# Two half batches by head parity, one transfer per unit of w_in and per phi, K or V load, and new sizes in the plan

## The chip, the core and the metric

The kernel runs on one core of one Trainium2 chip. The metric is the time of one execution in device microseconds (us); of the kernel before three runs are known, 734.42, 734.64 and 735.23, with the median 734.64. Five engines work side by side: TensorE (PE, its weight loads PEld), VectorE (DVE), ScalarE (ACT), GpSimd (POOL) and SyncE (SP), which here only issues transfers. A transfer runs on the core's 16 DMA engines.

## The reference

```
# q, k, v: 8 x 8 x 576 x 64, phi: 8 x 8 x 576 x 32   (batch, head, token, ...)
a    = softmax of phi over the tokens
k_m  = einsum('bhsm,bhsd->bhmd', a, k)          # 32 x 64 per head
v_m  = einsum('bhsm,bhsd->bhmd', a, v)
attn = softmax(q @ k_m.T / 8)                   # 576 x 32 per head
x    = (attn @ v_m), heads side by side         # 4608 x 512
h    = x @ w_in                                 # w_in 512 x 2048
out  = (relu(h) ** 2) @ w_out                   # w_out 2048 x 512
```

The weights w_in and w_out arrive as 64-bit floats, so each is 8 MB. The other inputs are 32-bit.

## The kernel before, in words

**The mathematics is folded.** Since x is attn times v_m, the kernel never forms x: it multiplies v_m by w_in once per batch (VW, function `vw`) and then h is attn times VW. `attention_turned` (batches 0 and 1) and `attention` (2 to 7) make attn, turned so that the memory slots lie on the partitions, as a high part `ath` and a rest `atl`. `mm1` makes h as three products (high by high, rest by high, high by rest), 12 matmuls of 288 columns for one slice of 128 columns of w_in; ACT and DVE make relu and square, again as a high part `gh` and a rest `glo`. `mm2` adds the slice to four accumulators, 12 matmuls of 512 columns; `mm2_left` does the left-over 64 tokens of two batches. There are 16 slices in each of 8 batches. Slices go first through 4 of batch 0, then the 16 of batch 1, then the other 12 of batch 0, then batch 2 and on.

**The weights.** `decode` loads a unit of 128 rows by 512 numbers (0.52 MB in 64 bit) into a buffer `raw` and makes 32-bit floats with some six DVE and ACT instructions. There are 16 units of w_in (`piece("wi", j)`, four for each quarter j) and 16 of w_out. The units of w_in come as two transfers, one to partitions 0 to 63 and one to 64 to 127, since a tile holds heads 0 to 3 in its lower 64 partitions and heads 4 to 7 in its upper 64. Units of w_out come as one transfer to 128 partitions.

**The inputs of a batch.** Batches 0 and 1 are computed in two halves of four heads (`memory_half`, hh 0 and 1), with tokens on the partitions; phi, K, V and q of a half come as a transfer to 128 partitions and a small one for the left-over 64 tokens. In batches 2 to 7 `memory` loads phi, K and V with `rows`, two transfers of 64 partitions each.

**The order of the work.** Every step is recorded as an operation with the engines that may do it and a cost. `Plan.order` gives each operation a rank from the table PLACES and plays the program through with these costs; the start times that come out set the order in which each engine's instructions are written, and which engine does a step where it has a choice. A load counts its `size` as time on the wire, `size / WIRE`, after FIRST ns. Where the play leaves TensorE idle, `emit` writes `fill` matmuls of 512 columns on zeros, one for each 260 ns of the gap: into a bank nobody reads (L472), or adding zero to a live accumulator (L474). The fills do no work of the reference. Waits at run time are by semaphores; each engine does its instructions in the order written, and SP issues the transfers in the order written as well.

The first h of the program (`h_0`, batch 0) needs `ath` and `atl` of both halves, that is: q of the second half, its scores `psc`, its softmax on DVE and ACT, a transpose `pat` and two evictions. It also needs VW of the first quarter of w_in, that is its four units.

Of the kernel before, what the change touches and what calls it, by code (L numbers as in the profile page):

```python
# [27 lines left out]
FIRST = 1100  # L28
# [360 lines left out]
def tile_attention_moe(  # L389
# [90 lines left out]
    seq += [(b, f) for b in range(2, B) for f in range(NFF)]  # L480


    w_in_u = w_in.bitcast(U32).rearrange("(r s d) (f t) -> r d s f t", r=2, d=D, t=2)
    w_out_u = w_out.bitcast(U32).rearrange("(j p) (e t) -> p j e t", p=P, t=2)
    wi = {}
    wo = {}

    def decode(kind, j, h, room):
# [4 lines left out]
        def load(d):  # L493
# [3 lines left out]
            for r in (0, 1):  # L497
                d(R()[64 * r:64 * r + 64].rearrange("p (f t) -> p f t", t=2), w_in_u[r][:, h, j * ND:(j + 1) * ND, :])
# [652 lines left out]
```

## Time and profile before

| what | value |
|---|---|
| median of three runs | 734.64 us |
| the profiled execution, its own time | 732.51 us |
| its span on the core | 730.7 us |
| TensorE busy | 717.7 us, 98% |
| VectorE busy | 488.8 us, 67% |
| ScalarE busy | 323.0 us, 44% |
| granted TensorE clock, mean | 1.00 of full speed |
| read from memory, written | 56.10 MB, 9.44 MB |

The span runs from the first to the last instruction; 1.8 us of the profiled execution lie outside it. The share of TensorE holds the fill matmuls as busy time, and matmuls overlap in the pipeline, so that the mean of one is longer than the distance from one to the next. A share over the whole span hides that the program has two parts: until about 140 us weights are loaded and decoded, after that they are at hand.

### The profile page before, as it was taken

What the parts mean: (1) busy time and instruction counts of PE and PEld (TensorE: products, weight loads), DVE (VectorE), ACT (ScalarE), POOL (GpSimd) and SP (SyncE); (2) the same over time, 40 slices, a digit from 0 to 9 for tenths busy, and PEclk for the clock granted to TensorE, in tenths of its full rate; (3) what the DMA queues carried; (4) which work ended last, traced back from release to release, by engine and by line L of the source; (5) the groups of instructions that cost most, each with busy time, mean ns of one, the idle gap of its engine ahead of it and who ended that gap; (6) DMA issues with size and microseconds to landing.
All of it is one profiled execution on the core that took longest, in us unless ns stands there. A gap on an engine that the chain in (4) does not pass through costs nothing.

```text
span 730.7 us, 13856 instructions
## 1 busy us (share of the span) xinstructions
PE 717.7 (98%) x5440; PEld 580.5 (79%) x5445; DVE 488.8 (67%) x1153; ACT 323.0 (44%) x737; POOL 53.4 (7%) x116
## 2 busy tenths in 40 slices
PE   8899899999999999999999999999999999999997
PEld 4577688787788878888888888887888888888886
DVE  3899999943684559666884358855795357764541
ACT  3577997753551335323452235533443134343230
POOL 1000000010001000120004100040004100040000
PEclk9999999999999999999999999999999999999999
DMA  9995444496314342035304421145314010020002
GB/s 238 267 249 138 144 146 118 138 214 157 82 31 117 84 98 62 14 103 136 92 1 118 119 62 31 32 116 122 77 31 109 23 32 1 1 58 1 1 0 73
DMA packets 46241, 66.44 MB, mean 91 GB/s; under 512 B 9760, under 2 KB 33312, under 8 KB 46176
## 3 DMA queue, kind: packets, MB, share of 16 engines
q1 hardware_dynamic: 42144, 56.77, 30.9%
q0 software_dynamic: 3552, 8.13, 4.0%
q8 instruction: 43, 0.70, 0.4%
q10 hardware_dynamic: 480, 0.66, 0.3%
q14 instruction: 22, 0.18, 0.1%
HBM read 56.10 MB, written 9.44 MB: 90 GB/s over the span
## 4 chain that ended last, share of the span: by engine, by line
PE 84%; DVE 5%; DMA 2%; ACT 2%; issue 1%; SPq 0%; DVEq 0%; ACTq 0%
PE h L944 25%; PE acc L982 15%; PE acc L979 15%; PE acc L980 15%; PE accl L1005 6%; PE vwpv L836 4%; DMA raw<-in_moe_w_in_dram 2%; PE pkv_pa L593 1%; DVE work L512 1%; PE pscpa L876 1%; PE pkv_pv L593 1%; DVE work L520 1%; DMA raw<-in_moe_w_out_dram 1%; DVE work L511 0%; DVE work L509 0%
## 5 line engine op out<-in xcount | busy, mean ns | idle before, releaser
L944 PE MATMUL h<-ath,vw 128*128 128x288 f32 x1024 | 212.3, 296 | 0.5 <-ACT vw L446 0.5
L979 PE MATMUL acc<-wo,gh 128*128 128x512 f32 x512 | 203.8, 398 | 0.0
L980 PE MATMUL acc<-wo,gh 128*128 128x512 f32 x512 | 201.2, 393 | 0.0
L944 PEld LDWEIGHTS h<-ath,vw 128*128 128x128 f32 x1024 | 172.0, 188 | 19.4 <-ACT vw L446 1.4
L982 PE MATMUL acc<-wo,glo 128*128 128x512 f32 x512 | 181.1, 398 | 1.5 <-DVE glo L954 1.5
L950 ACT ACTIVATE gh<-r 128x512 fp32r<-128x512 f32 x128 | 80.6, 630 | 116.9 <-PE acc L980 81.0
L979 PEld LDWEIGHTS acc<-wo,gh 128*128 128x128 f32 x512 | 96.1, 188 | 28.0 <-issue 10.6
L982 PEld LDWEIGHTS acc<-wo,glo 128*128 128x128 f32 x512 | 93.8, 188 | 28.9 <-issue 9.6
L944 PE MATMUL h<-atl,vw 128*128 128x288 f32 x512 | 109.5, 295 | 0.0
L980 PEld LDWEIGHTS acc<-wo,gh 128*128 128x128 f32 x512 | 96.1, 188 | 16.5
L954 DVE TENSOR_TENSOR glo<-r,gh 128x512 fp32r<-128x512 f32 x128 | 87.5, 684 | 23.9 <-PE acc L982 19.1
L948 ACT ACTIVATE r<-h 128x288 f32<-128x288 f32 x146 | 58.7, 408 | 80.2 <-PE h L944 63.1
L949 DVE TENSOR_SCALAR r<-h 128x288 f32<-128x288 f32 x110 | 50.2, 456 | 64.0 <-PE h L944 62.3
L944 PEld LDWEIGHTS h<-atl,vw 128*128 128x128 f32 x512 | 82.1, 188 | 0.0
L1041 POOL DMA_DIRECT2D out_dram<-o x84 | 41.6, 502 | 476.1 <-DVE o L446 261.9
L953 DVE TENSOR_TENSOR r<-r 128x576 f32<-128x576 f32 x54 | 40.5, 758 | 40.7 <-ACT gh L950 30.8
L951 ACT ACTIVATE gl<-r 128x64 fp32r<-128x64 f32 x128 | 32.0, 252 | 58.0 <-DVE r L949 48.4
L952 ACT ACTIVATE r<-r 128x576 f32<-128x576 f32 x74 | 50.5, 685 | 1.6
L1005 PE MATMUL accl<-wo,gl 128*128 128x512 f32 x192 | 47.2, 393 | 0.0
L1005 PEld LDWEIGHTS accl<-wo,gl 128*128 128x128 f32 x192 | 35.6, 188 | 7.5
L955 DVE TENSOR_TENSOR gl<-r,gl 128x64 fp32r<-128x64 f32 x128 | 27.5, 218 | 9.5 <-ACT r L952 8.3
L446 ACT CAST vw<-vwpa 128x256 fp32r<-128x256 f32 x50 | 17.2, 377 | 32.0 <-PE vwpa L836 31.7
(157 smaller groups left out, 724.0 us busy)
## 6 DMA issues: line engine op xcount, KB each, us to landing
q<-in_q_dram SPq DMA_DIRECT2D x96, 136.0 KB, 2.9
raw<-in_moe_w_in_dram SPq DMA_DIRECT2D x32, 256.0 KB, 4.3
raw<-in_moe_w_out_dram SPq DMA_DIRECT2D x16, 512.0 KB, 3.5
out_dram<-o POOLq DMA_DIRECT2D x80, 64.0 KB, 2.9
KV<-in_v_dram SPq DMA_DIRECT2D x12, 320.0 KB, 6.6
KV<-in_k_dram SPq DMA_DIRECT2D x12, 320.0 KB, 6.3
phi<-in_phi_dram SPq DMA_DIRECT2D x12, 288.0 KB, 5.3
KV<-in_k_dram SPq DMA_DIRECT2D x12, 256.0 KB, 5.3
```

The costliest lines, as they stand in the source:

```text
L944: nc.tensor.matmul(p()[:, 0:n], V()[:, l, hh, c0:c0 + P], x()[:, hh, cs], start=(i == 0), stop=(i == 5))
L948: op({"ACT": act(n), **({} if b < 2 else {"DVE": tt(n)})}, lambda e, cs=cs, n=n, p=p: nc.scalar.activation(r()[:, cs], p()[:, 0:n], AF.Rel ...
L949: else nc.vector.tensor_scalar(r()[:, cs], p()[:, 0:n], 0.0, None, ALU.max), [p], [(r, h)])
L950: op({"ACT": act(SM)}, lambda e: nc.scalar.activation(gh(), r()[:, 0:SM], AF.Square), [r], [gh])
L952: op({"ACT": act(S), **({} if b < 2 else {"DVE": tt(S)})}, lambda e: nc.scalar.activation(r(), r(), AF.Square) if e == "ACT" else nc.vecto ...
L953: else nc.vector.tensor_mul(r(), r(), r()), [r], [r], port=BOTH)
L954: vec({"DVE": tt(SM)}, lambda e: nc.vector.tensor_sub(glo(), r()[:, 0:SM], gh().bitcast(F32)), [r, gh], [glo])
L979: nc.tensor.matmul(a(), gh()[:, c], t()[:, 0], start=f0, stop=False)
L980: nc.tensor.matmul(a(), gh()[:, c], t()[:, 1], start=False, stop=False)
L982: nc.tensor.matmul(a(), glo()[:, c], t()[:, 0], start=False, stop=f1)
L1005: nc.tensor.matmul(a(), G()[:, l, :], t()[:, w], start=(ff == 0 and n == 0), stop=(ff == NFF - 1 and n == 2))
L1041: d(rows, o()[32 * j:32 * (j + n), :])
```

## The change

The halves of a batch become the heads of one parity: half hh holds heads hh, hh + 2, hh + 4 and hh + 6 (`heads`). A pair of neighbouring heads then lies on partitions 0 to 63 and 64 to 127 of one tile. In w_in the 128 rows of two neighbouring heads are contiguous, and in phi, K and V so are their tokens; a unit of w_in and a load of phi, K or V in `memory` becomes one transfer to 128 partitions. Sizes in the plan are other numbers, FIRST goes from 1100 to 1400, and the table PLACES is new throughout. The arithmetic of every step stays as it was.

```diff
-FIRST = 1100
+FIRST = 1400
 PLACES = (
-    8, 1, 3, 9, 5, 15, 18, 19, 20, 21, ...
...
-    w_in_u = w_in.bitcast(U32).rearrange("(r s d) (f t) -> r d s f t", r=2, d=D, t=2)
+    w_in_u = w_in.bitcast(U32).rearrange("(s p) (f t) -> p s f t", p=P, t=2)
...
-            for r in (0, 1):
-                d(R()[64 * r:64 * r + 64].rearrange("p (f t) -> p f t", t=2), w_in_u[r][:, h, j * ND:(j + 1) * ND, :])
+            d(R().rearrange("p (f t) -> p f t", t=2), w_in_u[:, h, j * ND:(j + 1) * ND, :])
...
-        dma(load, 450000, w=[rk], two=kind == "wi", lead=True)
+        dma(load, 400000 if kind == "wi" else 335000, w=[rk], lead=True)
...
     def heads(x, b, hh):
 
-        return x[b, 4 * hh:4 * hh + 4]
+        return x[b].rearrange("(s r) n w -> r s n w", r=2)[hh]
 
     def rows(d, dst, src, lo, hi):
 
         w = src.shape[3]
-        for x in (0, 1):
-            d(dst[64 * x:64 * x + 64].rearrange("p h c w -> p h (c w)"),
-              src[0, 4 * x:4 * x + 4].rearrange("h (p c) w -> p h (c w)", c=RC)[:, :, lo * w:hi * w])
+        d(dst.rearrange("p h c w -> p h (c w)"),
+          src[0].rearrange("(s r) n w -> s (r n) w", r=2).rearrange("s (p c) w -> p s (c w)", c=RC)[:, :, lo * w:hi * w])
...
-        dma(lambda d: rows(d, a(), phi[b:b + 1], 0, RC), 807000, [], [A], two=True, lead=True)
+        dma(lambda d: rows(d, a(), phi[b:b + 1], 0, RC), 650000, [], [A], lead=True)
...
-        dma(lambda d: tokens(d, a(), heads(phi, b, hh)), 468000, [], [(A, (hh, "in"))], two=True, lead=True)
+        dma(lambda d: tokens(d, a(), heads(phi, b, hh)), 333000, [], [(A, (hh, "in"))], two=True, lead=True)
...
-            dma(load, 689000, [], [Q, QL], two=True, lead=True)
+            dma(load, 551000, [], [Q, QL], two=True, lead=True)
...
-                        src = q[b, 4 * hh + 2 * y:4 * hh + 2 * y + 2].rearrange("a (p c) d -> p a (c d)", c=NC)
+                        src = heads(q, b, hh)[2 * y:2 * y + 2].rearrange("a (p c) d -> p a (c d)", c=NC)
```

What the new plan does with the order is seen at three places. Line numbers after the change are two lower in most of the program. In all, the program has 79 fill matmuls before (74 ahead of the first h, 5 later) and 54 after, all ahead of the first h; all other matmuls are the same in number and shape. DVE has 14 instructions more and ACT 14 fewer, among them nine squares `r<-r` of batches 2 to 7 and six casts `vw<-vwpv` more on DVE.

SP, the start of the program, from the first half's inputs of batch 0 to the first unit of w_out; `KV_1` and `q_1` belong to the second half. Before:

```order
L498 DMA raw<-in_moe_w_in_dram 64x1024 x2
L639 DMA KV_1_84<-in_k_dram 128x4x256
L640 DMA KV_1_84<-in_k_dram 64x4x64
L639 DMA KV_1_84<-in_v_dram 128x4x256
L640 DMA KV_1_84<-in_v_dram 64x4x64
L752 DMA q_1_251<-in_q_dram 128x4x256
L753 DMA ql_1_253<-in_q_dram 64x4x64
L498 DMA raw<-in_moe_w_in_dram 64x1024 x4
L495 DMA raw<-in_moe_w_out_dram 128x1024
L639 DMA phi_350<-in_phi_dram 128x4x128
```

After:

```order
L497 DMA raw<-in_moe_w_in_dram 128x1024 x2
L637 DMA KV_1_86<-in_k_dram 128x4x256
L638 DMA KV_1_86<-in_k_dram 64x4x64
L637 DMA KV_1_86<-in_v_dram 128x4x256
L638 DMA KV_1_86<-in_v_dram 64x4x64
L497 DMA raw<-in_moe_w_in_dram 128x1024
L750 DMA q_1_256<-in_q_dram 128x4x256
L751 DMA ql_1_258<-in_q_dram 64x4x64
L495 DMA raw<-in_moe_w_out_dram 128x1024
L637 DMA KV_0_217<-in_k_dram 128x4x256
L638 DMA KV_0_217<-in_k_dram 64x4x64
L637 DMA phi_338<-in_phi_dram 128x4x128
```

All four units of the first quarter of w_in now stand ahead of `q_1`, where two stood before, and a K of batch 1 stands ahead of that batch's first phi.

DVE, the softmax of the second half of batch 0 (`rz_1`, `S_1`), shortly ahead of the first h; the row `work<-raw` belongs to the decoding of weights. Before:

```order
L667 TENSOR_TENSOR mx_0_437<-mx_0_437,phi_350 128x128
L446 CAST vw_0_462<-vwpv_0_443 128x256
L740 TENSOR_REDUCE rz_1_467<-S_1_453 128x16
L846 TENSOR_TENSOR vw_0_462<-vwpa_0_445,vw_0_462 128x256
L741 TENSOR_SCALAR rz_1_467<-rz_1_467 128x16
L846 TENSOR_TENSOR vw_1_465<-vwpa_0_445,vw_1_465 128x256
L846 TENSOR_TENSOR vw_0_462<-vwpv_0_443,vw_0_462 128x256
L511 TENSOR_SCALAR work<-raw 128x512
L742 RECIPROCAL rz_1_467<-rz_1_467 128x16
L846 TENSOR_TENSOR vw_1_465<-vwpv_0_443,vw_1_465 128x256
L743 TENSOR_TENSOR S_1_453<-S_1_453,rz_1_467 128x512
```

After:

```order
L665 TENSOR_TENSOR mx_0_438<-mx_0_438,phi_338 128x128
L844 TENSOR_TENSOR vw_0_445<-vwpa_0_427,vw_0_445 128x256
L736 TENSOR_TENSOR rest_208<-rest_208,redl_447 128x128
L738 TENSOR_REDUCE rz_1_454<-S_1_440 128x16
L844 TENSOR_TENSOR vw_1_456<-vwpa_0_427,vw_1_456 128x256
L739 TENSOR_SCALAR rz_1_454<-rz_1_454 128x16
L844 TENSOR_TENSOR vw_0_445<-vwpv_0_425,vw_0_445 128x256
L740 RECIPROCAL rz_1_454<-rz_1_454 128x16
L669 TENSOR_REDUCE mc_0_477<-pmx_0_474 128x1
L741 TENSOR_TENSOR S_1_440<-S_1_440,rz_1_454 128x512
```

A cast of VW, one subtraction of VW and an instruction of the decoding have left this stretch; the row on `rest` and the one on `mc_0` stood a little later before.

PE, the third VW of batch 0 (`vw_4`) and the first h that reads it. Before:

```order
L836 MATMUL vwpa_4_2229<-wi_1239,VT_221 32x512
L979 MATMUL acc_4_2_2090<-wo_1164,gh_2197 128x512
L980 MATMUL acc_4_2_2090<-wo_1164,gh_2197 128x512
L982 MATMUL acc_4_2_2090<-wo_1164,glo_2211 128x512
L474 LDWEIGHTS zero
L474 MATMUL acc_4_0_2080<-zero 128x512
```

After:

```order
L980 MATMUL acc_4_2_2042<-wo_1172,glo_2075 128x512
L980 MATMUL acc_4_0_2035<-wo_1133,glo_2179 128x512
L977 MATMUL acc_4_3_2046<-wo_1133,gh_2161 128x512
L978 MATMUL acc_4_3_2046<-wo_1133,gh_2161 128x512
L980 MATMUL acc_4_3_2046<-wo_1133,glo_2179 128x512
L977 MATMUL acc_4_1_2059<-wo_1133,gh_2161 128x512
L978 MATMUL acc_4_1_2059<-wo_1133,gh_2161 128x512
L980 MATMUL acc_4_1_2059<-wo_1133,glo_2179 128x512
L942 MATMUL h_1_2203<-ath_407,vw_4_2183 128x288 x2
```

Before, three matmuls of the second product and four fills, of which the first is shown, stand between the last matmul of VW and the h, and one more fill a little later. After, twelve matmuls of the second product stand there, of which the last eight are shown, and no fill.

## Rows read from the trace of the kernel before

**Rows 1.** The page: span, and busy time of each engine.

```profile
span 730.7 us, 13856 instructions
PE 717.7 (98%) x5440; PEld 580.5 (79%) x5445; DVE 488.8 (67%) x1153; ACT 323.0 (44%) x737; POOL 53.4 (7%) x116
```

**Rows 2.** Windows by stretch; columns in the first line.

```profile
core 0: us, PE busy (x) PEld busy (x) DVE busy (x) ACT busy (x) POOL busy (x), PEclk, DMA share, GB/s
0.00:40.60 40.60, 34.90 (x337) 19.46 (x341) 26.94 (x70) 16.90 (x35) 4.63 (x18) 1.00 0.99 256
40.60:75.00 34.40, 33.15 (x360) 26.29 (x359) 33.36 (x84) 28.32 (x66) 0.00 (x0) 1.00 0.68 173
75.00:140.00 65.00, 63.00 (x382) 51.78 (x374) 63.08 (x146) 56.07 (x126) 0.00 (x0) 1.00 0.50 145
...
182.00:725.00 543.00, 543.00 (x3980) 448.60 (x3979) 344.77 (x808) 200.36 (x463) 46.50 (x94) 1.00 0.24 61
```

**Rows 3.** Windows, fills of L472 alone: busy and count of PE, PEld.

```profile
0.00:40.60 40.60, 20.10 (x70) 7.78 (x74) 1.00 0.99 256
```

**Rows 4.** Timeline of PE: start, length in us, instruction, idle before it.

```profile
24.91 1.09 PE L764 MATMUL pq<-ident,q 128*128 128x128 f32 x8 [0.42 <-DMA q<-in_q_dram]
...
29.30 2.00 PE L792 MATMUL psc<-kb,qT 128*128 128x64 f32 x16 [1.28 <-ACT kb L446]
```

**Rows 5.** Timeline of PE, around the first h.

```profile
39.66 1.04 PE L472 MATMUL idle<-zero 128*128 128x512 bf16 x4
40.83 1.30 PE L687 MATMUL pkv<-KV,phi 128*32 128x128 f32 x40
```

**Rows 6.** DMA from 21 to 26.5 us: packets; queue, MB, share of engines.

```profile
DMA packets 404, 1.25 MB, mean 228 GB/s; under 512 B 83, under 2 KB 109, under 8 KB 403
...
q1 hardware_dynamic: 403, 1.24, 102.6%
```

**Rows 7.** DMA from 35 to 37 us, the same view.

```profile
DMA packets 231, 0.77 MB, mean 385 GB/s; under 512 B 33, under 2 KB 48, under 8 KB 231
...
q1 hardware_dynamic: 231, 0.77, 102.6%
```

**Rows 8.** DMA from 7 to 12 us, packets, bytes and share.

```profile
q1 hardware_dynamic: 2274, 1.55, 113.2%
```

**Rows 9.** DMA from 53 to 57 us, packets, bytes and share.

```profile
q1 hardware_dynamic: 602, 0.87, 100.2%
```

**Rows 10.** Timeline of SP: issue of w_in's fourth unit, batch 1's phi.

```profile
17.82 1.72 SPq L498 DMA_DIRECT2D raw<-in_moe_w_in_dram  x2
24.88 0.63 SPq L640 DMA_DIRECT2D phi<-in_phi_dram  x1
```

**Rows 11.** DMA issues from 18.4 to 19 and 24.8 to 25.4 us: us to landing.

```profile
raw<-in_moe_w_in_dram SPq DMA_DIRECT2D x2, 256.0 KB, 10.9
...
phi<-in_phi_dram SPq DMA_DIRECT2D x1, 32.0 KB, 7.0
```

**Rows 12.** Timeline of DVE, from 27 to 41 us.

```profile
27.63 0.43 DVE L509 TENSOR_SCALAR work<-raw 128x512 f32<-128x512 f32 x1 [1.61 <-DMA raw<-in_moe_w_in_dram]
27.98 0.42 DVE L511 TENSOR_SCALAR work<-raw 128x512 uint32<-128x512 uint32 x1
...
33.10 0.42 DVE L665 TENSOR_TENSOR mx<-phi 128x256 f32<-128x256 f32 x1
...
40.06 0.68 DVE L812 TENSOR_TENSOR atl<-pat,ath 128x512 fp32r<-128x512 f32 x1
```

**Rows 13.** Timeline around the third VW of batch 0.

```profile
174.33 0.59 PE L836 MATMUL vwpa<-wi,VT 64*32 64x512 f32 x1
...
175.88 0.82 PE L474 MATMUL acc<-zero 128*128 128x512 bf16 x3
...
176.35 0.61 PE L944 MATMUL h<-ath,vw 128*128 128x288 f32 x2
```

**Rows 14.** The page's costliest groups: the square on DVE.

```profile
L953 DVE TENSOR_TENSOR r<-r 128x576 f32<-128x576 f32 x54 | 40.5, 758 | 40.7 <-ACT gh L950 30.8
```

More of the change, by code (lines that the diff above doesn't have):

```diff
@@ L610, in memory @@
             for i, src in ((0, k), (1, v)):
-                dma(lambda d, i=i, src=src, kv=kv, lo=lo, hi=hi, n=n: rows(d, kv()[:, i, :, 0:n], src[one], lo, hi), 937000 if n == 5 else 603000, [], [(KV, i)], two=True, lead=True)
+                dma(lambda d, i=i, src=src, kv=kv, lo=lo, hi=hi, n=n: rows(d, kv()[:, i, :, 0:n], src[one], lo, hi), 742000 if n == 5 else 580000, [], [(KV, i)], lead=True)
             def mm(e, kv=kv, lo=lo, hi=hi):
@@ L658, in memory_half @@
         for i, src in ((0, k), (1, v)):
-            dma(lambda d, i=i, src=src: tokens(d, kv()[:, i], heads(src, b, hh)), 689000, [], [(KV, i)], two=True, lead=True)
+            dma(lambda d, i=i, src=src: tokens(d, kv()[:, i], heads(src, b, hh)), 551000, [], [(KV, i)], two=True, lead=True)
         kin = [(A, (hh, "pad")), (A, (hh, "in"))]
```

282 rows, old and new, of the table PLACES are left out of this document.

## The prediction

> **What bounds the kernel now.** I read the page's table of engines first: TensorE is busy for 717.7 of 730.7 us [rows 1]. Then the windows by stretch, which show where the other 13 us lie and what the share hides [rows 2]. From 182 to 725 us TensorE is busy for all of 543.00 us; its matmuls are the same in number and shape after the change, so nothing is to be won there, only to be lost. Up to 40.60 us it is busy for 34.90, but 20.10 of these are fills [rows 3], 74 by the weight loads, some 0.27 us each. Real work is 34.90 - 20.10 = 14.8 us, and 25.8 us are fill or idle. From 40.60 to 140 us the idle time is 1.25 + 2.00 = 3.25 us, with VectorE busy for 96.4 of 99.4 us beside it: there two engines are nearly full.
>
> So the question is what sets the end of the fills, at 39.66 + 1.04 = 40.7 us [rows 5]. In the same window the DMA engines are busy for 0.99 of the time: the front is bound by transfers. The DMA views of short stretches say at what rate. From 21 to 26.5 us the engines are full, the packets are mainly the 4 KB ones of w_in, and 1.24 MB move: 0.225 MB/us [rows 6]. From 35 to 37 us they are just as full, again with 4 KB packets, now of w_out, and 0.77 MB move: 0.385 MB/us [rows 7]. Loads of K, V and q in 1 KB pieces make 1.55 MB in 5 us, 0.310 MB/us [rows 8]. What differs between w_in and w_out is that a w_in transfer fills 64 partitions and a w_out transfer 128; the phi of batch 2, also in transfers of 64 partitions, is in the stretch with 0.218 MB/us [rows 9].
>
> The timelines tie this to the first h. The last two halves of w_in, issued from 17.82 us, land 10.9 us after issue [rows 10, 11], the last at about 29.4 us with its issue 0.6 later. VectorE idles 1.61 us for w_in until 27.63 [rows 12] and from then on is full until the first h: it reaches batch 1's phi at 33.10 and ends `atl` of the second half of batch 0 at 40.06 + 0.68 = 40.7. That, not TensorE, sets the 40.7 us.
>
> **The change, part by part.** *One transfer per unit of w_in.* A unit is 0.524 MB: 2.33 us at 0.225 MB/us, 1.36 at the rate of w_out, 1.69 at that of K. The new transfer has the form of w_out's (128 partitions, 4 KB each), so I take 1.36, with 1.69 and 2.33 as the other bounds. Four units stand ahead of the first h: 4 x 0.97 = 3.9 us less transfer time (2.6 at K's rate, 0 at the old one).
>
> The Trainium skill, SBUF — State Buffer, section A bandwidth-pool intuition that's wrong, gives about 358 GB/s from memory to one core. By that figure a unit would need 1.46 us, four of them 0.4 us more, and the sum below would be 4.9 instead of 5.3. The stretch of w_out at 385 GB/s lies above the figure, and the measurement decides.
>
> *The order on SP.* All four units now stand ahead of the second half's q. In the old order the transfers up to the fourth unit were done at 29.4; the same bytes are now done at 29.4 - 3.9 = 25.5, and q comes last of them. It landed at 24.9 before [rows 4], so q itself is 0.6 later. Behind it follow a unit of w_out (1.36), a K half of 0.59 MB (1.90) and phi of 0.295 MB (0.95): batch 1's phi lands at 25.5 + 4.2 = 29.7 us, before at 24.88 + 7.0 = 31.9. At K's rate for w_in it would be 31.0.
>
> *What VectorE does with it.* The subtraction of the second half's softmax stands right behind batch 1's first maximum, before and after, so it waits for this phi and for the scores. Before, the scores began 29.30 - 24.91 = 4.4 us after q, 1.28 of it waiting for `kb` [rows 4]; K and V of that half now come well ahead of q, so I count 3.1, and 1.0 for the eight score matmuls (half of the 2.00 us of sixteen records): 25.5 + 4.1 = 29.6, the same time as phi. From that maximum to the end of `atl` VectorE needed 40.7 - 33.1 = 7.6 us without a gap. Three instructions have left this stretch, each about 0.34 us from start to start (27.63 to 27.98): 6.6 us remain. The end of `atl` comes at 29.8 + 6.6 = 36.4, or at 37.7 with phi at 31.0, against 40.7. That is 4.3 or 3.0 us. I take 4.0, near the row of the transfer of the same form. The fills are an independent check: there are 20 fewer ahead of the first h, 20 x 0.27 = 5.4 us. They free time only if what follows is ready, so 5.4 is the upper end and nothing is the lower: idle time would stand where the fills stood. Two small steps of batch 1's memory on TensorE (1.30 us of `pkv` among them) move from just ahead of the first h to just behind it; both orders do them without a gap there, so they cost nothing either way.
>
> *The five fills near 176 us.* Three take 0.82 us [rows 13], five take 1.35. They covered the wait of h for the evictions of `vw_4`: from the last VW matmul at 174.33 to the h at 176.35 are 2.0 us. Twelve matmuls of the second product now stand there, of 512 columns like a fill; at a fill's 0.27 us they take 3.2 us, more than the wait. I take 1.3 us of gain; if `vw_4` is late anyway, none.
>
> *The rest of the weights.* The other 12 units of w_in gain up to 0.97 us each in the stretch where VectorE is 97% busy. VectorE's work there is the same and starts earlier by what the first h gains, so I count nothing; bounds are the 3.25 us of idle that could vanish and as much again that could appear. *Single transfers of phi, K and V in batches 2 to 7, fewer issues on SP:* hidden under 543 us of full TensorE, with the DMA engines at 0.24; nothing. If that cover went, a load late by a microsecond would cost a microsecond. *Nine squares of 758 ns [rows 14] and some casts more on VectorE:* 9 x 0.758 = 6.8 us and a little, on an engine with 344.8 of 543 us busy; nothing, and up to 1 us per batch if they stand ahead of something that TensorE waits for.
>
> Sum: -4.0 - 1.3 = -5.3 us, from a span of 730.7 to 725.4, and from the profiled 732.5 to 727.2. The profiled execution lies 2.1 us below the median of the runs; from 734.64 the same difference gives 729.3.
>
> **The rivals.** *w_in stays slow.* If its source, rows cut out of a wide matrix, sets 0.225 MB/us and not the 64 partitions, q lands at 29.4 instead of 24.9 and phi at 33.6; `atl` ends at 33.7 + 6.6 = 40.3. The fills that are gone become idle time, and 0.4 + 1.3 = 1.7 us remain: 733.0. For it: w_out is read in one piece, w_in not. Against it: phi, from another source, is as slow in halves, and K in 128 partitions is not.
> The Trainium skill, SBUF — State Buffer, section Door 1: The DMA port swizzle, says that a transfer of 64 partitions reaches half of the ports that one of 128 reaches. By that rule this rival falls away and the forecast's rate holds; the trace agrees, with 0.225 and 0.218 against 0.385 and 0.310 MB/us.
>
> *VectorE keeps its pace.* Between 40.6 and 140 us it has 3.0 us to spare in 99.4. If decoding ends no earlier because w_out, whose transfers are unchanged, or a free `raw` buffer paces it, half of the gain comes back as idle of TensorE: 4.0 / 2 + 0.7 = 2.7 us less, 732.0. For it: 97% busy. Against it: its whole list shifts with the front.
>
> *Slower: the new order opens waits in the full stretch.* TensorE idles 0.0 us there now. The squares that moved to VectorE put 0.76 us ahead of rests and casts that the next product needs. If every one of the six batches 2 to 7 lost 1.2 us, that would be 7.2 against 5.3 won: 736.5. It decides from 0.9 us per batch. Against it: VectorE is 63% busy there, and the new program has no fill left behind the first h.
>
> *More than forecast.* All 5.4 us of the fills, 1.3, and the 3.25 us of idle up to 140 us: 734.6 - 9.9 = 724.7.
>
> **How the numbers follow.** Forecast 0.64, w_in stays slow 0.12, VectorE keeps its pace 0.12, slower 0.07, more 0.05. A change under 0.2% (1.5 us: below 733.2 is faster, above 736.1 slower) can't be told from none. Faster: 0.64 + 0.12 + 0.05 and 0.05 of the first rival, whose 733.0 lies at the edge, 0.86; the other 0.07 of it is no change; slower 0.07. The forecast's own range, from 3.0 + 0 to 5.4 + 1.3 and 1 us of idle, is 734.6 - 7.7 = 726.9 to 734.6 - 3.0 = 731.6; to leave out no more than two in ten it reaches to the two rivals near it, 725.8 to 733.0.
>
> **What would show it.** In the profile after: w_in stretches at about 0.38 MB/us with full engines; the fills end near 36.7 us; batch 1's phi is reduced near 30; no wait of h for `vw` near 172 us; no idle TensorE from there to the end. Wrong it would be if the fills ended after 39 us, or if TensorE idled over 5 us between there and 140 us, or at all in the long stretch.

## The result and the profile after

The changed kernel takes 727.34 us (median of 4 runs, 726.74 to 727.61) against 734.93 us of the kernel before, run beside it on the same chip (4 runs, 734.42 to 737.02): a ratio of 0.989, 95% interval 0.987 to 0.9911. The forecast was 729.3 us, within 725.8 to 733.0. The sign and the place were those forecast; the gain is about 2 us larger than the sum of 5.3, and one step of the path to it is not the one that the traces show.

The profiled execution itself took 727.61 us, span 725.8, where that of before took 732.51 and 730.7. Its difference, 4.9 us, is close to the sum. The page's first lines after, which answer to [rows 1]:

```profile
span 725.8 us, 13697 instructions
PE 711.7 (98%) x5416; PEld 578.7 (80%) x5420; DVE 498.6 (69%) x1167; ACT 317.7 (44%) x723; POOL 53.9 (7%) x116
```

The windows by stretch after, to be held against [rows 2]: stretch and its length, busy time and count of each engine, granted clock, DMA share, GB/s.

```profile
0.00:36.60 36.60, 31.00 (x316) 18.21 (x320) 25.70 (x69) 17.35 (x37) 5.27 (x18) 0.95 1.01 277
36.60:75.00 38.40, 35.05 (x373) 28.54 (x372) 36.40 (x92) 30.81 (x71) 0.00 (x0) 1.00 0.60 174
75.00:140.00 65.00, 64.15 (x390) 52.08 (x390) 63.11 (x148) 56.56 (x127) 0.00 (x0) 1.00 0.43 138
182.00:720.00 538.00, 538.00 (x3952) 444.06 (x3951) 354.54 (x818) 190.67 (x440) 46.32 (x94) 1.00 0.22 61
```

The first row ends 4 us earlier than its counterpart and moves 277 GB/s instead of 256, at full DMA engines in both. The second and third hold 3.35 + 0.85 = 4.2 us of idle TensorE, about a microsecond more than before. The last is full, as before. The fills of L472 in the first stretch (busy time and count of PE, of PEld), beside [rows 3]:

```profile
0.00:36.60 36.60, 15.78 (x50) 5.74 (x54) 0.95 1.01 277
```

By the weight loads 54 instead of 74, as the order had them. TensorE's timeline at their end, beside [rows 5]: start, length, instruction, idle time before it.

```profile
35.36 1.25 PE L472 MATMUL idle<-zero 128*128 128x512 bf16 x5
36.94 0.51 PE L679 MATMUL pkv<-ones,phi 128*32 128x1 f32 x40 [0.33 <-ACT phi L673]
37.38 0.54 PE L942 MATMUL h<-ath,vw 128*128 128x288 f32 x2
```

And VectorE's, beside [rows 12]:

```profile
30.01 0.41 DVE L663 TENSOR_TENSOR mx<-phi 128x256 f32<-128x256 f32 x1
...
36.35 0.66 DVE L810 TENSOR_TENSOR atl<-pat,ath 128x512 fp32r<-128x512 f32 x1
36.92 0.28 DVE L741 TENSOR_TENSOR rest<-rest,rzl 128x128 f32<-128x128 f32 x1
38.21 0.43 DVE L508 TENSOR_SCALAR work<-raw 128x512 f32<-128x512 f32 x1 [1.01 <-DMA raw<-in_moe_w_out_dram]
```

Batch 1's phi is reduced at 30.01 (before 33.10), `atl` ends at 37.0 (before 40.7), the fills end at 36.6. Between them VectorE is full but for 0.27 us ahead of a maximum at 31.69, and it comes to the phi at 30.01 without a wait. The first h of before, which [rows 5] leave out, stood at 42.25:

```profile
42.25 0.51 PE L944 MATMUL h<-ath,vw 128*128 128x288 f32 x2
```

The row at 38.21 is new: VectorE now waits for a unit of w_out, 1.01 us, which it did not before.

The DMA engines from 13 to 15 us, where most packets are the 4 KB ones of single w_in transfers, beside [rows 6, 7]: packets, bytes, share of 16 engines.

```profile
DMA packets 229, 0.71 MB, mean 357 GB/s; under 512 B 38, under 2 KB 58, under 8 KB 229
...
q1 hardware_dynamic: 229, 0.71, 101.9%
```

That is 0.35 MB/us where w_in in halves had 0.225. The Trainium skill, SBUF — State Buffer, section A bandwidth-pool intuition that's wrong, puts memory to one core at about 358 GB/s; this stretch lies at that figure, the one of [rows 7] above it.

### The profile page after: what moved, and what is told of

Same layout as the page of the kernel before. It is cut to its first block, busy times and chain, and to the rows that moved or that the text cites. A ratio compares the mean times of both kernels' runs of the same rounds, so it can differ in the third digit from the quotient of the medians.

```text
span 725.8 us, 13697 instructions
## 1 busy us (share of the span) xinstructions
PE 711.7 (98%) x5416; PEld 578.7 (80%) x5420; DVE 498.6 (69%) x1167; ACT 317.7 (44%) x723; POOL 53.9 (7%) x116
## 4 chain that ended last, share of the span: by engine, by line
PE 90%; DMA 4%; DVE 2%; ACT 2%; SPq 1%; issue 1%; ACTq 0%
PE h L942 27%; PE acc L980 16%; PE acc L977 16%; PE acc L978 16%; PE accl L1003 6%; PE vwpv L834 4%; DMA raw<-in_moe_w_out_dram 2%; PE pkv_pa L591 1%; DMA KV<-in_k_dram 1%; PE pscpa L874 1%; PE pkv_pv L591 1%; PE psc L790 1%; ACT work L509 0%; DVE work L508 0%; DVE work L511 0%
## 5 line engine op out<-in xcount | busy, mean ns | idle before, releaser
L980 PE MATMUL acc<-wo,glo 128*128 128x512 f32 x512 | 185.1, 398 | 0.6 <-DVE glo L952 0.6
L951 DVE TENSOR_TENSOR r<-r 128x576 f32<-128x576 f32 x63 | 47.5, 757 | 40.6 <-ACT gh L948 32.2
L950 ACT ACTIVATE r<-r 128x576 f32<-128x576 f32 x65 | 44.5, 685 | 1.5
L446 ACT CAST vw<-vwpa 128x256 fp32r<-128x256 f32 x52 | 17.6, 377 | 29.4 <-PE vwpa L834 28.7
```

Of the source, the lines that this page charges most:

```text
L950: op({"ACT": act(S), **({} if b < 2 else {"DVE": tt(S)})}, lambda e: nc.scalar.activation(r(), r(), AF.Square) if e == "ACT" else nc.vecto ...
L951: else nc.vector.tensor_mul(r(), r(), r()), [r], [r], port=BOTH)
L980: nc.tensor.matmul(a(), glo()[:, c], t()[:, 0], start=False, stop=f1)
```

## The experiments

Each time is a median. The kernel before gave 734.36 us (19 runs) beside the first four runs, 733.52 (16) beside the next four, 733.37 (35) beside the last four; it scatters by 4.0 to 4.3 us beside the first two groups and by 7.5 beside the third, so the ratios say more than one difference. The changed kernel was run again only in the first group. Where a kernel of the other two is set against its 727.2 us, the ratios would make it 1.2 to 2.6 us slower still; no sign below depends on this. "Behind the changed kernel" is said of the same matmuls in the two traces.

**The changed kernel again, and its two halves.** `after_again` has no edit.

> The changed kernel itself once more, as the base of this group. The medians so far differ by 7.6 us, the two profiled executions by 4.9 (732.5 and 727.6). Theory: the difference that the traces show, 5 us, is the change, and the other 2.5 us are scatter of the kernel before, whose profiled execution was 2 us under its median; then before minus after lies between 5 and 7.5 us here. Rival: the profile hides a part of the gain; then it is 7 to 8 again and both profiled executions lie on their medians.

727.18 us (725.13 to 727.72), ratio 0.9886 [0.9861, 0.991]. The result repeats. A difference of 7.2 us lies in the theory's 5 to 7.5 as in the rival's 7 to 8, so it does not choose between them; this kernel's new profiled execution, 727.37, lies on its median.

`a_split_wi` gives back the halves of w_in alone:

```diff
-            d(R().rearrange("p (f t) -> p f t", t=2), w_in_u[:, h, j * ND:(j + 1) * ND, :])
+            for r in (0, 1):
+                pr = slice(64 * r, 64 * r + 64)
+                d(R()[pr].rearrange("p (f t) -> p f t", t=2), w_in_u[pr, h, j * ND:(j + 1) * ND, :])
```

> The changed kernel, but a unit of w_in comes again in two transfers of 64 partitions, from the same rows of w_in and in the same order on all engines. Theory, the 64 partitions are what is slow: w_in moves at about 0.22 MB/us again, the four first units take 2.6 to 3.9 us longer, the fills end at 39 to 40.5 instead of 36.6 us, and the time is 2 to 4 us above the changed kernel. Rival, the source's rows set the rate: no more than 0.5 us, from the second issue on SP.

737.17 us, ratio to before 1.0031 [1.0011, 1.005]: 10.0 us above the changed kernel, over twice what was expected. Its DMA engines from 14 to 17 us, the bytes nearly all in 4 KB packets of w_in's halves:

```profile
DMA packets 211, 0.68 MB, mean 228 GB/s; under 512 B 44, under 2 KB 44, under 8 KB 211
...
q1 hardware_dynamic: 211, 0.68, 105.9%
```

0.68 / 3 = 0.227 MB/us: the old rate with the new order. The first h stands at 42.44 us, 5.1 behind the changed kernel; by 60 us it is 8 us behind, by 150 us 10.

`c_old_transfers` keeps only the new order and its measured sizes; all transfers, and with them which heads lie in which half, are the old ones; two of its edits, the others undo `w_in_u`, `rows` and the load of q in the same way:

```diff
-        return x[b].rearrange("(s r) n w -> r s n w", r=2)[hh]
+        return x[b, 4 * hh:4 * hh + 4]
...
-            d(R().rearrange("p (f t) -> p f t", t=2), w_in_u[:, h, j * ND:(j + 1) * ND, :])
+            for r in (0, 1):
+                d(R()[64 * r:64 * r + 64].rearrange("p (f t) -> p f t", t=2), w_in_u[r][:, h, j * ND:(j + 1) * ND, :])
```

> The changed kernel's table of places, sizes and FIRST, with all transfers and the halves of heads as before the change. Theory: TensorE idles where the fills were, the fills end at 39.5 to 41 us, the first unit of batch 0 comes no sooner; only the five later fills are won: 1 to 2.5 us under before. It should lie within 1 us of the changed kernel with split w_in, as the parity of heads and the loads of batches 2 to 7 cost nothing. Rival, the order alone makes the gain: within 1 us of the changed kernel.

736.75 us, ratio 1.003 [1.0012, 1.0049]. It is within 0.4 us of `a_split_wi`: the parity of the heads and the single loads of phi, K and V in batches 2 to 7 cost and give nothing beyond the scatter of these medians, some 1 to 1.5 us, and w_in's halves are what matters among the transfers.

`b_old_order` is the opposite: the new transfers with the old table PLACES, and

```diff
-FIRST = 1400
+FIRST = 1100
...
-        dma(load, 400000 if kind == "wi" else 335000, w=[rk], lead=True)
+        dma(load, 450000, w=[rk], two=kind == "wi", lead=True)
```

and the other old sizes.

> The kernel before with the new transfers and the parity of heads, but its own table of places, sizes and FIRST, so that order and fills stay as they were. Theory, the transfers bring the data sooner and the order has to be made for it: w_in at 0.38 MB/us, but the 74 fills stay; with 0.9 + 20.1 + 14.8 the fills can't end before 35.9 us, I expect 37 to 39 instead of 40.7, and the five later fills stay; time 1.5 to 3.5 us under before. Rival, the order alone makes the gain: within 1 us of before. Rival, the transfers alone make it: within 1 us of the changed kernel.

730.26 us, ratio 0.9931 [0.9909, 0.9953]. TensorE at the end of its fills:

```profile
37.05 1.25 PE L472 MATMUL idle<-zero 128*128 128x512 bf16 x5
38.43 0.84 PE L685 MATMUL pkv<-KV,phi 128*32 128x128 f32 x21
```

So the transfers alone bring 4.1 us (734.36 to 730.26), 2.4 of them by the end of the fills (38.3 instead of 40.7). The order alone costs 2.4 us (734.36 to 736.75); on top of the new transfers it brings 3.1 (730.26 to 727.18). It is an order that pays only with fast transfers.

**Is it the 64 partitions, or w_in's source?** `d_split_wo` halves w_out instead, which is read in one piece.

```diff
-                d(R().rearrange("p (f t) -> p f t", t=2), w_out_u[:, 2 * j + h])
+                for r in (0, 1):
+                    pr = slice(64 * r, 64 * r + 64)
+                    d(R()[pr].rearrange("p (f t) -> p f t", t=2), w_out_u[pr, 2 * j + h])
```

> The changed kernel, but each w_out unit comes in two transfers of 64 partitions (w_in stays in one of 128). Theory (the 64 partitions of a transfer set its rate): although w_out is read in one piece, a stretch with nothing but w_out packets moves about 0.22 MB/us instead of 0.385, a unit takes about 2.3 us instead of 1.36; batch 1's phi, behind three of these units, lands 1 to 3 us later, and the whole takes 3 to 10 us more, near 730 to 737. Rival (w_in was slow because its rows are cut out of a wide matrix): w_out keeps 0.35 MB/us or more, and the time stays within 1.5 us of 727.2.

738.67 us, above the 730 to 737 expected, but from a single run, so that the time proves little; the rate does not depend on it. Its DMA engines from 34 to 35 us, when the only 4 KB packets are w_out's:

```profile
DMA packets 76, 0.20 MB, mean 201 GB/s; under 512 B 17, under 2 KB 31, under 8 KB 76
...
q1 hardware_dynamic: 76, 0.20, 96.4%
```

Full engines at 0.20 MB/us (0.24 from 33.5 to 35 us, where 0.36 MB move), against 0.385 for the same matrix in 128 partitions [rows 7]. The source is not it; a transfer of 64 partitions has little more than half the rate. By the Trainium skill, SBUF — State Buffer, section Door 1: The DMA port swizzle, it reaches half of the ports; the trace agrees.

**Where the 10 us of the halves arise.** `h_split_first` halves only the four units ahead of the first h, `i_split_later` only the twelve behind it:

```diff
+            if j == 0:
+                for r in (0, 1):
+                    pr = slice(64 * r, 64 * r + 64)
+                    d(R()[pr].rearrange("p (f t) -> p f t", t=2), w_in_u[pr, h, j * ND:(j + 1) * ND, :])
+                return
```

and the same with `if j > 0`.

> The changed kernel, with only the first four units of w_in (those ahead of the first h) in two transfers of 64 partitions; the other twelve stay single. With all sixteen halved the time was 737.2, 10.0 us above the changed kernel, of which 5.0 stood at the first h and the rest came up to 150 us. Theory (the prediction's count: the four units ahead of the first h are the whole worth of the single transfers, and what comes later in the halved run is their backlog in the queue): 8 us or more of the 10.0, 735 to 737.5. Rival (each group pays by itself): first h 4 to 5 us later, at about 42, and no more behind it: 731 to 732.5.

> The changed kernel, with only the last twelve units of w_in (from 40 us on) in two transfers of 64 partitions; the first four stay single. Theory (the prediction counted nothing for these twelve): first h unchanged at 37 to 38 us, time within 1 us of 727.2. Rival (where VectorE is 97% busy, a late unit is not made good): 3 to 5 us slower, 730 to 732.5, with TensorE's idle time between 40 and 150 us longer by that.

731.56 us (ratio 0.9962 [0.9946, 0.9978]) and 733.47 us (0.9988 [0.9965, 1.0012]): 4.4 and 6.3 us above the changed kernel's 727.2, together 10.7, against the 10.0 of `a_split_wi`; in the traces 3.9 and 5.9 us at 150 us, together 9.8 against 10.4. In `h_split_first` the rival held: the matmuls are 4.0 us behind at the first h and 3.9 to 4.5 from there to the end. In `i_split_later` the theory fell, but the loss lies above the rival's 730 to 732.5 and is not all idle time. The first h is where it was (37.69), and one place, from 47 to 54 us, costs 5.0 of the 5.9. VectorE there:

```profile
46.35 0.69 DVE L957 TENSOR_TENSOR glo<-r,gh 128x512 fp32r<-128x512 f32 x1
50.15 0.43 DVE L513 TENSOR_SCALAR work<-raw 128x512 f32<-128x512 f32 x1 [3.12 <-DMA raw<-in_moe_w_out_dram]
```

TensorE there, in `i_split_later`:

```profile
52.55 0.47 PE L715 MATMUL pvt<-ident,kx 128*128 128x128 f32 x1 [3.61 <-ACT kx L701]
...
54.90 1.05 PE L767 MATMUL pq<-ident,q 128*128 128x128 f32 x4
...
58.54 2.00 PE L795 MATMUL psc<-kb,qT 128*128 128x64 f32 x16
```

The same in the changed kernel:

```profile
50.40 0.33 PE L710 MATMUL pvt<-ident,kx 128*128 128x128 f32 x1 [1.11 <-ACT kx L696]
...
51.70 0.64 PE L762 MATMUL pq<-ident,q 128*128 128x128 f32 x4
...
53.87 2.00 PE L790 MATMUL psc<-kb,qT 128*128 128x64 f32 x16
```

The releaser of VectorE's wait is a unit of w_out, which was not touched: it is issued at 42.0 us (42.4 in the changed kernel) behind a w_in unit in halves, whose second half lands at 48.1 instead of 46.3, and is at hand 2.1 us later. VectorE takes its instructions in order, so `rs` behind the decoding waits too, then `kx` on ScalarE, then `pvt` on TensorE: 3.61 us instead of 1.11, 2.15 later by the clock of the trace. The matmuls between `pvt` and `psc` then take 2.5 us more (58.54 - 52.55 against 53.87 - 50.40), and the windows say why:

```profile
47.00:51.00 4.00, 1.94 (x24) 1.22 (x15) 0.89 (x3) 0.80 (x2) 0.00 (x0) 1.00 0.99 234
51.00:52.00 1.00, 0.00 (x0) 0.00 (x0) 0.97 (x5) 0.95 (x3) 0.00 (x0) 0.71 0.87 210
52.00:56.00 4.00, 3.45 (x15) 3.34 (x16) 3.31 (x8) 2.57 (x8) 0.00 (x0) 0.50 0.13 35
```

During the 3.6 us without work the granted clock falls to 0.50, which is 1.2 GHz, and stays there behind it. The wait is paid twice: 2.5 us more of idle time, 2.5 us in slow matmuls behind it.

**The fills and the clock.** `f_no_fills` leaves out all fill matmuls; `e_more_fills` adds six ahead of the first transposes of q, where TensorE idles 1.0 us in the changed kernel.

```diff
-            fill(int(o.gap / (FILL if o.start > LEAD else 400)))
+            fill(0)
```

```diff
-                op({"PE": 440}, mm, [Q], [pq], lead=True, code=8, mode=1)
+                first = op({"PE": 440}, mm, [Q], [pq], lead=True, code=8, mode=1)
+                if u == "0_0" and x == 0:
+                    more[first] = 6
...
-            fill(int(o.gap / (FILL if o.start > LEAD else 400)))
+            fill(int(o.gap / (FILL if o.start > LEAD else 400)) + more.get(o, 0))
```

> The changed kernel without any fill matmul; the rest of the program is the same. It shows what the fills are worth and whether their number can be read as time. Theory (fills only stand in time that is idle anyway, but keep the granted clock up): from 10 to 40 us the clock falls to 0.5 in most stretches, the real matmuls there take up to twice their time, and the end of the first h comes 2 to 5 us later; the time is 729 to 733. Rival (transfers and VectorE set the first h, whatever TensorE's clock): first h within 0.7 us of 37.4, time within 1 us of 727.2.

> The changed kernel with six more fill matmuls ahead of the first transposes of batch 0's q, where TensorE idles 1.0 us for the transfer of q just before its granted clock falls to 0.50. Theory (the idle time ahead brings the fall, and the fall costs nothing that the end waits for, because VectorE sets the end of the fills): the granted clock from 10 to 20 us is 1.00 instead of 0.83, the 40 pkv take 1.3 us instead of 2.4, and the time stays within 0.7 us of 727.2. Rival 1 (the slow pkv delay rs and with it what follows): 1.0 us faster, 726.2. Rival 2 (the fall has another cause): clock stays at 0.83 and the fills cost up to 1 us.

Without fills: 733.81 us, ratio 1.0002 [0.9986, 1.0018], at the edge of the 729 to 733 expected. All of the change's gain goes, though the fills do no work of the reference. TensorE without fills:

```profile
19.81 3.52 PE L790 MATMUL psc<-kb,qT 128*128 128x64 f32 x16
...
25.24 2.36 PE L685 MATMUL pkv<-KV,phi 128*32 128x128 f32 x40 [0.28 <-DVE rs L690]
...
42.50 0.85 PE L942 MATMUL h<-ath,vw 128*128 128x288 f32 x2
```

In the changed kernel the same `psc` take 1.90 us (from 17.84) and the same `pkv` 1.30 (from 21.67), and the first h stands at 37.38. Only the `psc` from 31.97 us on take 1.90 here too. With six more: 727.97 us (726.69 to 728.07), ratio 0.9924 [0.9903, 0.9944]; no gain. The changed kernel from 13 to 15 us, and then `e_more_fills` from 13 to 17 (columns as above):

```profile
13.00:14.00 1.00, 0.92 (x20) 0.95 (x24) 0.17 (x1) 0.00 (x0) 0.00 (x0) 0.50 1.04 338
14.00:15.00 1.00, 1.00 (x25) 0.98 (x20) 0.62 (x2) 0.00 (x0) 0.00 (x0) 0.50 1.00 377
```

```profile
13.00:17.00 4.00, 3.41 (x49) 1.88 (x49) 2.30 (x9) 1.11 (x4) 0.52 (x1) 1.00 1.05 361
```

The six fills keep the clock at 1.00 and the first 40 `pkv` at 1.30 us, which take 2.36 in the changed kernel. TensorE then only waits longer for what comes next, because transfers and VectorE set the pace up to the first h. So the fall of the clock in this place, over by 17 us, costs nothing, matmuls that stay slow up to 31 us (`f_no_fills`) go with a first h 5 us later, and a fall behind 50 us (`i_split_later`) costs all that the matmuls lose.

**The five late fills.** `k_no_late_fills` is the kernel before without them:

```diff
-            fill(int(o.gap / (FILL if o.start > LEAD else 400)))
+            if o.start < 100000:
+                fill(int(o.gap / (FILL if o.start > LEAD else 400)))
```

> The kernel before, without its five fill matmuls near 176 us; nothing else is changed. Theory (they stood in a wait of h for the evictions of vw_4, and what the change won there is the twelve matmuls of the second product that it puts in the wait): the wait shows as 1 to 2 us of idle TensorE at 175 us, and the time is within 0.5 us of the kernel before. Rival (vw_4 was there in time, and the fills themselves were the loss): no idle there, 1.0 to 1.4 us faster than the kernel before.

732.46 us, ratio 0.9983 [0.9968, 0.9999], 1.2 us with an interval of 0.1 to 2.3. TensorE at the place, beside [rows 13]:

```profile
173.57 0.61 PE L836 MATMUL vwpa<-wi,VT 64*32 64x512 f32 x1
174.11 0.50 PE L979 MATMUL acc<-wo,gh 128*128 128x512 f32 x1
174.45 0.39 PE L980 MATMUL acc<-wo,gh 128*128 128x512 f32 x1
174.68 0.40 PE L982 MATMUL acc<-wo,glo 128*128 128x512 f32 x1
174.91 0.42 PE L944 MATMUL h<-ath,vw 128*128 128x288 f32 x2
```

No idle time before h: `vw_4` was there. The rival held: the fills covered nothing, they were the loss. (The granted clock of this trace is 0.95 nearly throughout; its length is not compared.)

**Can the new waits be had back?** In the changed kernel TensorE waits 0.41 us for `rs` at 38.6 and 1.11 for `kx` at 49.3, both behind a decoding step that waits for w_out. `g_scalings_first` moves the small instructions ahead of these steps:

```diff
...
-        for o in plan.order():
+        ops = plan.order()
+        ops = moved(ops, tags["max", "1_1"] + tags["rs", "1_0"][:1])
+        ops = moved(ops, tags["rs", "1_1"] + [tags["kx", "1_1", i] for i in (0, 1)])
+        for o in ops:
```

> The changed kernel, but two groups of small instructions stand ahead of a decoding step that waits for its weights: on VectorE the third maximum of batch 1's second half and rs of the first half (ahead of the decoding that idles 1.0 us for w_out at 38.2 us), and rs of the second half with its two scalings kx on ScalarE (ahead of the one that idles 0.6 us at 48.0). Theory (TensorE's waits of 0.4 us for rs at 38.3 and 1.1 us for kx at 48.9 come only from that order): both waits go and the time is 1 to 2 us less, 725.2 to 726.2. Rival (VectorE, 97% busy up to 140 us, sets the pace, and the time comes back as waits for vw or S between 50 and 140 us): within 0.5 us of 727.2.

727.55 us (727.07 to 731.01), ratio 0.9927 [0.9906, 0.9949]: nothing. Both waits are gone, and one of the same size stands a little later:

```profile
51.92 0.66 PE L765 MATMUL pq<-ident,q 128*128 128x128 f32 x4 [1.09 <-ACT kb L446]
```

`l_sub_on_pool` takes work from VectorE instead: the sixteen subtractions that end the decoding of a w_out unit run on GpSimd.

```diff
-        vec({"DVE": tt(ND)}, lambda e: nc.vector.tensor_sub(part(1), wf(), part(0).bitcast(F32)),
+        vec({"DVE": tt(ND)}, lambda e: nc.gpsimd.tensor_sub(part(1), wf(), part(0).bitcast(F32)),
```

> The changed kernel, with the sixteen subtractions that end the decoding of a w_out unit (128x512, 0.68 us each on VectorE, fifteen of them between 37 and 140 us) on GpSimd, which does nothing else there; the order on every engine is otherwise the same. Theory (VectorE, 97% busy, holds TensorE up for 3.4 us of idle time between 37 and 140 us): VectorE has 10 us less to do there, the idle time falls to 1 to 2 us, and the time is 1 to 2.5 us less, 724.7 to 726.2. Rival 1 (the waits there are for transfers and buffers, not for VectorE's capacity): within 0.7 us of 727.2. Rival 2 (GpSimd takes over twice as long for one, or slows VectorE while it works): wo comes late, 1 to 5 us slower.

733.09 us, ratio 0.9983 [0.9963, 1.0002]: 5.9 us slower than the changed kernel, past the 1 to 5 us of the second rival, whose two reasons both show. Groups of GpSimd from 37 to 140 us (busy time, mean ns of one, idle before):

```profile
L523 POOL TENSOR_TENSOR wo<-work,wo 128x512 fp32r<-128x512 f32 x14 | 20.2, 1448 | 88.0 <-ACT wo L446 65.2 <-DVE wo L446 22.8
```

Groups of VectorE in this kernel:

```profile
L511 DVE SCALAR_TENSOR_TENSOR work<-work 128x512 uint32<-128x512 uint32 x25 | 19.3, 772 | 1.0 <-ACT work L509 0.9
L508 DVE TENSOR_SCALAR work<-raw 128x512 f32<-128x512 f32 x26 | 13.1, 504 | 0.0
...
L519 DVE CUSTOM_DVE_ANT_0 work<-raw,work 128x1024 uint16<-128x1024 uint16 x14 | 12.1, 864 | 0.3
```

And in the changed kernel:

```profile
L511 DVE SCALAR_TENSOR_TENSOR work<-work 128x512 uint32<-128x512 uint32 x26 | 17.7, 682 | 0.6 <-ACT work L509 0.6
...
L508 DVE TENSOR_SCALAR work<-raw 128x512 f32<-128x512 f32 x26 | 10.9, 418 | 1.6 <-DMA raw<-in_moe_w_out_dram 1.6
L519 DVE CUSTOM_DVE_ANT_0 work<-raw,work 128x1024 uint16<-128x1024 uint16 x15 | 10.3, 686 | 0.0
```

One subtraction takes 1448 ns instead of 684, and with these on GpSimd VectorE's own instructions are longer, 90 to 180 ns each in the mean of these three groups: 25 x 0.09 + 26 x 0.086 + 14 x 0.178 = 7 of the 9.6 us taken off. TensorE waits for `wo` from GpSimd only 0.3 us in all; by which waits the 5.9 us come was not settled. No version tried is faster than the changed kernel.

## Why the prediction was right, point by point

- **The rate of a w_in unit: right, the value a little high.** Taken was 0.385 MB/us, measured 0.35, about 1.5 us for a unit instead of 1.36. The first rival, that the source sets the rate, falls with `d_split_wo`.
- **The first h: right in time, the path in part by luck.** Forecast and trace after: the second half's q at 25.5, its transposes start at 25.04 behind fills without a wait; batch 1's phi at 29.7, reduced at 30.01; `atl` ends at 36.4, measured 37.0, since from that maximum VectorE took 7.0 us and not 6.6; fills end at 36.7, measured 36.6. The term was -4.0; the first h itself moved from 42.25 to 37.38, 4.9 us. `b_old_order` has the fills end 2.4 us earlier by the transfers alone. But the step "so it waits for this phi and for the scores" is not what the traces show. After the change VectorE waits for no other engine and no transfer from 17.0 to 37.2 us; its own list, full since 17 us, brings it to phi. In the profiled execution of `after_again` this phi, issued at 24.20 and 24.63, lands by 29.4. The landing of its second part, VectorE's maximum and the last fills there:

```profile
phi<-in_phi_dram SPq DMA_DIRECT2D x1, 32.0 KB, 4.8
```

```profile
31.15 0.41 DVE L663 TENSOR_TENSOR mx<-phi 128x256 f32<-128x256 f32 x1
```

```profile
36.49 1.25 PE L472 MATMUL idle<-zero 128*128 128x512 bf16 x5
```

  The maximum comes 1.8 us after phi and the fills end at 37.7: the first half's q came later there (its first transposes start at 12.20 instead of 10.84), and VectorE's list with it. What the single transfers take away is VectorE's wait for w_in itself, 1.61 us before [rows 12]. With the first four units in halves again (`h_split_first`) it is back, and VectorE then reaches the maximum at 34.35, again without a wait for phi:

```profile
27.59 0.43 DVE L515 TENSOR_SCALAR work<-raw 128x512 uint32<-128x512 uint32 x1 [2.85 <-DMA raw<-in_moe_w_in_dram]
```

  So that phi lands just as VectorE reaches it is luck. Nor is the first h passed on as it stands: in `after_again` it comes at 38.52, 1.1 us later, and from 50 us on the matmuls stand within 0.3 us of where they stood in the first execution.
- **The fills as a check: right to distrust.** 20 fewer fills were read as 5.4 us at most. `f_no_fills` shows that a count of fills cannot be read as time at all: without its 54 fills the kernel is 6.6 us slower.
- **The five late fills: the size right, the reason wrong.** -1.3 was forecast, -1.2 measured in `k_no_late_fills`. But they covered no wait; the sentence that the twelve matmuls now fill it names a wait that was not there.
- **The rest of the weights at nothing: this step failed as a reason.** The prediction held that VectorE's list only shifts with the front. With halves in the new order these twelve units cost 6.3 us (`i_split_later`), outside the 3.25 taken as bound. In the profiled executions the matmuls lead by 4.5 to 4.9 us at the first h, by only some 1.5 to 3 between 44 and 75 us, where the new waits for w_out lie, and by 4.1 again at 110: the net is near zero, but because single transfers let the tighter order hold, not because nothing hangs on them. The rival "VectorE keeps its pace" described the dip and not the recovery.
- **The price of the first rival was wrong.** Had w_in stayed slow, the prediction gave 733.0; `a_split_wi` is that case, at 737.2. It counted the units ahead of the first h and left out the twelve later ones and the fall of the clock.
- **Batches 2 to 7 at nothing: right.** `c_old_transfers` and `a_split_wi` differ by 0.4 us, and TensorE has no idle time from 140 to 720 us. The rival of new waits there did not come.
- **The sum: 5.3 forecast, 4.9 between the two profiled executions, 7.2 to 7.6 between the medians.** The trace accounts for the 4.9: 3.7 at 170 us, 5.0 behind the late fills. The other 2 us lie in how the profiled execution was carried over to the median: that of before stands at the fast end of its own scatter (732.5 to 736.8 in 19 runs), those of the changed kernel, 727.6 and 727.4, on or just above its medians. What makes the kernel before scatter more was not settled; a fall of the clock like the one in `i_split_later` in some executions would do it, but no trace of before shows one.

## What to carry to other kernels

Where the DMA engines are full, divide bytes by time in stretches of one kind of transfer: here that showed a rate of 0.225 against 0.385 MB/us, and the partitions of a transfer, not its source, as the cause. What a faster transfer is worth depends on the order around it, so try the transfer, the order and both; here they gave -4.1, +2.4 and -7.2 us. A wait that an engine shares with what stands behind it in its list is priced by all of these, and a long one on TensorE, as the 3.6 us here, is paid again in slow matmuls. A row that comes at the time forecast does not yet show the path: look whether the engine waited there, and at a second execution.

## What was not expected of the hardware

- In a wait of TensorE of 3.6 us the granted clock fell to 0.50, which is 1.2 GHz, and stayed there for over 5 us, and matmuls that take 3.5 us from `pvt` to `psc` took 6.0. In the changed kernel the same fall stands from 13 to 16 us, after 1.0 and 0.4 us of idle time; six fills ahead of it keep 1.00.
- Without any fills `pkv` takes 2.36 us from 14.6 and again from 25.2 us, the length it has at 0.50 in the changed kernel, while the granted clock of these windows reads 1.00:

```profile
25.00:28.00 3.00, 2.36 (x40) 1.78 (x40) 2.98 (x8) 1.08 (x4) 0.17 (x2) 1.00 0.77 245
```

  The clock's column does not show this case; the lengths of the same instruction do. That it is the clock all the same is likely from the equal lengths, and not shown.
- A GpSimd subtraction of 128x512 takes 2.1 times VectorE's time and lengthens VectorE's instructions, but not all: L510, one input to 32-bit integers, stays at 423 ns. The Trainium skill, SBUF — State Buffer, section SBUF: two separate sides, has the two engines share one pair of ports as an exclusive lock, which some of VectorE's instructions need and others do not; the trace agrees in that three groups grow by 13 to 26% and L510 by nothing, but that the lock is the cause no run here shows.
